# A two-layer memory transformer on one core: the weighted values of all heads in one run, and their fill

## The chip, the cores and the metric

One core of a Trainium2 chip runs the kernel. The metric is the time of one execution on the device in microseconds; lower is better.

## The reference

Two layers, each an attention with a recurrent memory and a dense block, over x of 2048 tokens by 512.

```python
def _A_ref(x, mem0, Wq, Wk, Wv, Wo, seg_len):      # 64 segments of 32 tokens, memory of M = 8 rows
    mem = mem0
    for s in range(n_seg):
        h = jnp.concatenate([mem, xs], axis=1)      # L = 40 rows
        q, k, v = (jnp.einsum('btd,dhe->bhte', h, W) for W in (Wq, Wk, Wv))   # H = 32 heads of 128
        scores = jnp.where(mask, jnp.einsum('bhqe,bhke->bhqk', q, k) * scale, -1000000000.0)
        p = _softmax(scores, axis=-1)
        o = jnp.einsum('bhqk,bhke->bhqe', p, v)
        o = jnp.einsum('bhte,hed->btd', o, Wo)
        mem = o[:, :M, :].copy()                    # the next segment's memory
        outs.append(o[:, M:, :])

x = x + _A_ref(_layernorm(x), A_mem0, A_Wq, A_Wk, A_Wv, A_Wo, A_seg_len)
x = x + relu(_layernorm(x) @ w1) @ w2               # 512 -> 1376 -> 512
# and both lines once more: layer 1, with the same weights and the same first memory
```

A segment cannot start before the memory rows of the one before it are known.

## The kernel before

**Steps.** The kernel runs 68 steps. Step k works on segment k of layer 0 (called a = 0) and on segment k - 4 of layer 1 (a = 1, `DELTA = 4`), so that two recurrences share one program; from step 4 to 63 both are there. In the attention's tiles layer 0 has partitions 0 to 39 and layer 1 has 64 to 103. The engines' programs are in the order in which the source issues them (`manual_schedule`), apart from the blocks under `high_priority`, which stand in the same order here; GpSimd is free.

**One step on TensorE.** The heads go in two halves of 16 (`hf` 0 and 1):

1. `qk` of half 0 (L663, tiles `qp`), the values of the memory rows (`memory_values`, L332, tiles `vp`), in even steps `values1(k)`, and the scores of half 0 (`scores`, L703, banks `sp0` and `sp1`). The softmax of half 0 runs beside `qk` of half 1.
2. `transpose_p` (L747, tiles `tp` into `PT`) turns the probabilities `Pf` of half 0; then the scores of half 1; then `weighted_v(0)` (L762, tiles `pv`): 32 small matmuls, 16 heads by two layers, which read `Vs` and `PT`.
3. Work that does not belong to the chain of the step, as fill: `values1(k + 1)` in even steps, `values0(k + 3)` where `fills_v0(k)` holds, part of a dense block (`dense_h`, L589, tiles `hp`; `dense_y`, L610) or of an output projection (`output_x`, L460 and L463, tiles `wox`). Meanwhile the softmax of half 1 is made: `exponents` (maximum L718 and subtraction L721 on VectorE, exponential L729 on ScalarE) and `probabilities` (sum L735, reciprocal L736 on VectorE, product L738 into `Pf`: layer 0's on GpSimd, layer 1's on VectorE).
4. `transpose_p` of half 1, a second piece of fill, `weighted_v(1)`.
5. `output_mem` (L710): 32 matmuls of `OTm`, which holds the weighted values of the memory rows, with `Wo_sb`. Fill; the sum is copied to `wm_sb` (L1073, ScalarE), turned (`mt`, L1097) and copied to `HT` (L1100, VectorE), the next step's memory rows. Fill, and the next step.

**Which fill where.** `places(i)` cuts the 32 heads of pair i's output projection: in an even step, `wx[0:2]` stands ahead of the second transposition, `wx[1:3]` behind it, `wx[2:4]` behind `output_mem`, `wx[3:5]` behind `mt`. `hs` cuts the 11 parts of `dense_h` in the same way. Even steps are of two kinds. With k = 4n, an output projection of an odd pair is the fill. With k = 4n + 2, it is `dense_h` and, from 6 to 58, `values0` (16 matmuls a call, in four column groups of the array).

**Copies out of PSUM.** `outputs_m` (L785, ScalarE) copies the memory rows of a `pv` tile to `OTm`, 8 heads a copy; `outputs_x` (L793) the others to `OTx0` or `OTx1`: ScalarE for half 0, VectorE for half 1. `ahead(k, a)` gives how many rows go to `OTm`: 8, but 24 for layer 1 in steps 4n up to 60, where 16 token rows ride along in `output_mem`. In those steps `riders_add` (L562) follows on VectorE.

**Banks.** PSUM's eight banks are `ps_c` (three buffers in turn, for `qp`, `tp`, `mt`, the memory rows' `vp` and most `pv`), `ps_fill` (two, for fill and one `pv` of each half), `ps_wo` (one) and `sp0`, `sp1`. `output_mem` sums in `sp0`. A tile that takes a buffer waits for the copies of the tile that had it. `values0` uses `ps_c` for its first product and `ps_fill` for its second, whose copy to SBUF stands behind `transpose_p` of half 1 on ScalarE (`evict_v0`).

Of the kernel before, what the change touches and what calls it, by code (L numbers as in the profile page):

```python
# [7 lines left out]
BF = mybir.dt.bfloat16  # L8
F32 = mybir.dt.float32
# [8 lines left out]
DELTA = 4  # L18
# [4 lines left out]
def kernel(  # L23
# [34 lines left out]
    wk = ctx.enter_context(tc.tile_pool(name="wk", bufs=2))  # L58
    dram = ctx.enter_context(tc.tile_pool(name="vdram", bufs=2, space=DRAM))
    ps_c = ctx.enter_context(tc.tile_pool(name="ps_c", bufs=3, space=PSUM))  # L60
    ps_s = ctx.enter_context(tc.tile_pool(name="ps_s", bufs=1, space=PSUM))
    ps_wo = ctx.enter_context(tc.tile_pool(name="ps_wo", bufs=1, space=PSUM))
    ps_fill = ctx.enter_context(tc.tile_pool(name="ps_fill", bufs=2, space=PSUM))
# [140 lines left out]
    Vs = const.tile([128, H * Dh], BF)  # L204
# [3 lines left out]
    PT = const.tile([128, 8, 2, L], BF)  # L208
    OTx0 = const.tile([128, 2, H // 2, 128], BF)
    OTx1 = const.tile([128, H // 2, 128], BF)  # L210
    OTm = const.tile([128, H, 32], BF)
    hT = const.tile([128, NFC, 128], BF)

    sp_banks, sp_tiles = [], []
    for a in range(2):
        t = ps_s.tile([128, 512], F32, name=f"sp{a}")
# [4 lines left out]
    vmds, vds = {}, {}  # L221
# [105 lines left out]
    def group_values(lhsT, ii, dst, pool, tag, q, place="VmS", later=False):  # L327
        vp = pool.tile([128, 512], F32, tag=tag, name="vp")
        for c4 in range(NC4):
            for j in range(4):  # L330
                n = 4 * ii + j
                nc.tensor.matmul(vp[32 * j:32 * j + 32, :], lhsT=lhsT(c4), rhs=Wv_sb[:, c4, n * 512:(n + 1) * 512],  # L332
                                 start=(c4 == 0), stop=(c4 == NC4 - 1), tile_position=(0, 32 * j))

        def evict():
            VmS = wk.tile([128, 512], BF, tag=place, bufs=3 if place == "VmS" else 1, name="VmS")
            nc.scalar.copy(out=VmS[:], in_=vp[:])  # L337
            q.dma_start(out=dst[ii].rearrange("j t e -> (j t) e"), in_=VmS[:])

        if later:  # L340
            return evict
        evict()
# [8 lines left out]
    def values0(s, ii):  # L351

        if ii == 0:
            vds[0, s] = dram_values("vd0", "vd0", 4)
        t = tokens_T(s, 0, SEG)
        return group_values(lambda c4: t[:, c4, :], ii, vds[0, s], *((ps_fill, "fill") if ii else (ps_c, "c")), nc.sync,
                            "xn" if ii == 1 and s > 5 else "VmS", later=ii == 1 and s > 5)

    def values1(k, ii, place="VmS"):

# [58 lines left out]
    def fills_v0(k):  # L419

        return k % 2 == 0 and k + 3 < NSEG and k + 3 not in set_of

    def places(i):

        if i % 2 == 0:
            return (0, 10, 16, 24, H), (H,) * 5
        if i == NT - 1:  # L430
            return (0, 12, 12, 12, 12), (12, H, H, H, H)
        if fills_v0(2 * i + 2):
            return (0, 6, 10, 14, 20), (20, 23, 26, 30, H)
        return (0, 6, 10, 13, 16), (16, 23, 26, 30, H)

    def output_order(i):
# [202 lines left out]
    def block_normalize(b):  # L639
        dn["b"] = wk.tile([128, Dm], BF, tag="xn", bufs=1, name="xn")  # L640
        normalize(dn["b"], R_tiles[place(b)[0]], dn["x"])
# [96 lines left out]
        eng.tensor_tensor(out=P[:, :, 64 * a:64 * a + L], in0=es[:],  # L738
                          in1=sm[:].unsqueeze(2).to_broadcast([128, 8, L]), op=ALU.mult)

    def transpose_p():

        for p, copy in ((0, nc.vector.tensor_copy), (1, nc.scalar.copy)):
            tp = ps_c.tile([128, 4, 2, L], F32, tag="c")
            for sl in range(4):
                c = PL * (4 * p + sl)
                nc.tensor.matmul(tp[:, sl], lhsT=Pf[:, c:c + 128], rhs=ident_q, start=True, stop=True)  # L747
            copy(out=PT[:, 4 * p:4 * p + 4], in_=tp[:])  # L748

    def weighted_v(hf, act):  # L750
        pvs = {}
        for q in range(2):
            h0 = 16 * hf + 8 * q
            for a in act:
                pool, tag = (ps_fill, "fill") if (hf, q, a) in ((0, 0, 0), (1, 1, 1)) else (ps_c, "c")
                pvs[q, a] = pool.tile([128, 8, L], F32, tag=tag, name="pv")
            for hh in range(8):
                sl, g2 = divmod(8 * q + hh, 2)
                h = h0 + hh
                for a in act:  # L760
                    R = 64 * a
                    nc.tensor.matmul(pvs[q, a][:, hh, :], lhsT=Vs[R:R + L, h * Dh:(h + 1) * Dh],  # L762
                                     rhs=PT[R:R + L, sl, g2, :], start=True, stop=True)
        return pvs

# [11 lines left out]
    def ahead(k, a):  # L777

        return M + 16 if a == 1 and ride_of(k) is not None and ride_of(k)[2] == 0 else M

    def outputs_m(k, hf, pvs, q):
        for a in range(2):
            if (q, a) in pvs:
                h0, n = 16 * hf + 8 * q, ahead(k, a)
                nc.scalar.copy(out=OTm[:, h0:h0 + 8, a * M:a * M + n], in_=pvs[q, a][:, :, 0:n])  # L785

    def outputs_x(k, hf, pvs, q, copy, layers=(0, 1)):
        for a in layers:
            if (q, a) in pvs:
                h0, n = 16 * hf + 8 * q, L - ahead(k, a)  # L790
                c = 64 * a + SEG * (k % 2)
                ot = OTx1 if hf else OTx0[:, k // 2 % 2]
                copy(out=ot[:, 8 * q:8 * q + 8, c:c + n], in_=pvs[q, a][:, :, L - n:L])  # L793
# [7 lines left out]
    def step(k):  # L801
        act = [a for a in range(2) if 0 <= k - a * DELTA < NSEG]
        even = k % 2 == 0
        p = k // 2
        w = p - 1 if even and p >= 1 else None
        nw = p if not even else None
        dw = p - 1 if not even and p >= 1 else None
        first = dw is not None and dw < NP
# [168 lines left out]
        wo = sp_banks[0]  # L977
        with tc.high_priority(offset=PRIO):
            transpose_p()
            scores(qks[:2], act)  # L980
            scores(qks[2:], act)
            pvs = weighted_v(0, act)

            outputs_x(k, 0, pvs, 0, nc.scalar.copy)
            outputs_m(k, 0, pvs, 0)
            ess = exponents(act)


# [10 lines left out]
        if not apart:  # L999
            v1(1)  # L1000
        with tc.high_priority(offset=PRIO):
            outputs_m(k, 0, pvs, 1)
            outputs_x(k, 0, pvs, 1, nc.scalar.copy)
        v0(0)
        evict_v0 = v0(1)
        if k == 2:
            set_values(4, 3, 5)
            set_products(4, 5)
            set_store(4, nc.sync, 2, 4)
        hs = (0, 0, 4, 8, NFC) if fills_v0(k) else (0, 6, 8, 8, NFC) if len(act) == 1 else (0, 8, NFC, NFC, NFC)  # L1010
        if sooner is not None:
            dense_h(sooner, *hs[0:2])
        final = k == NSTEP - 1
# [6 lines left out]
        with tc.high_priority(offset=PRIO):  # L1020
            for a in act:
                probabilities(1, ess, a, k)
            if first:
                hand_on(dw)
            transpose_p()
            if evict_v0 is not None:
                evict_v0()
            if k == 0:
                set_evict(3, 4)
                set_products(3, 5)  # L1030
            if k == 1:
                set_evict(4, 2)
            if k == 2:
                set_evict(4, 5)
                set_products(4, 6)
            if first:
                block_moments(dw)
# [6 lines left out]
        if nw is not None:  # L1044
            output_x(nw, *nx[1:3])
        with tc.high_priority(offset=PRIO):
            pvs = weighted_v(1, act)
            for q2 in range(2):
                if cont:
                    outputs_m(k, 1, pvs, q2)  # L1050
            head = act[:1] if nx is not None and nw % 2 == 0 else act
            outputs_x(k, 1, pvs, 0, nc.scalar.copy if final else nc.vector.tensor_copy, head)
            if first:
                block_normalize(dw)
            outputs_x(k, 1, pvs, 1, nc.vector.tensor_copy, head)
            for q2 in range(2):
                outputs_x(k, 1, pvs, q2, nc.vector.tensor_copy, [a for a in act if a not in head])
            if back is not None and place(back)[1]:
                riders_add(back)
            if dw is not None and dw >= 3 and not final:  # L1060
                store(dw)
            if k == 2:
                set_evict(4, 6)
            if k == 0:
                set_evict(3, 5)
                set_values(3, 6, 7)
                output_mem(wo, 0, 24)
                set_values(3, 7, 8)
                output_mem(wo, 24, H)
            elif cont:  # L1070
                output_mem(wo, 0, H)
            if cont:
                nc.scalar.copy(out=wm_sb[:], in_=wo[:])  # L1073
            if k == 0:
                set_products(4, 0)
            if k == 2:
                set_products(4, 7)
# [125 lines left out]
```

## Time and profile before

| | |
|---|---|
| median of 3 runs | 1613.6 us (1612.4 to 1614.39) |
| the profiled execution | 1612.95 us; its span 1611.2 us |
| TensorE (PE) busy | 1597.3 us, 37172 matmuls |
| VectorE (DVE) busy | 1082.3 us |
| ScalarE (ACT) busy | 859.1 us |
| GpSimd (POOL) busy | 267.6 us |
| HBM | 69 GB/s over the span |

PE stands for matmuls, PEld for the loads of their stationary operand. The ends of matmuls are modelled and overlap, so what is read off here are their starts. A step takes some 22 to 24 us. A wait before a matmul is booked on the weight load ahead of it where that load reads what was waited for.

### The profile page before, as it was taken

The page shows a single profiled execution, that of the slowest core. Times are in us where ns is not written, and L with a number is a line of the kernel's source. Part 1 is how long each engine was busy: PE and PEld are TensorE (multiplying, and loading weights), DVE is VectorE, ACT ScalarE, POOL GpSimd, SP SyncE. Part 2 cuts the span into 40 slices and gives each one's busy share as a digit, 9 for nine tenths or more (in the row PEclk, how much of TensorE's full clock was granted, in tenths as well). Part 3 has the DMA queues.
Part 4 walks back from the last instruction along what each step waited for, and adds up shares of the span by engine and source line. Part 5 has one row for each costly group of instructions (what it writes and reads, how often), then busy time and mean ns, then how long its engine had stood idle before and what let it go on. Part 6 is the DMA issues. An engine that isn't in the chain of part 4 may idle for free.

```text
span 1611.2 us, 83133 instructions
## 1 busy us (share of the span) xinstructions
PE 1597.3 (99%) x37172; PEld 1175.3 (73%) x37172; DVE 1082.3 (67%) x2603; ACT 859.1 (53%) x2422; POOL 267.6 (17%) x510
## 2 busy tenths in 40 slices
PE   9999999999999999999999999999999999999998
PEld 4677777677777767777777777777777777777766
DVE  5556766776776677677667767666766767676655
ACT  4455555555555555555555555555555555555544
POOL 1112111111211111121111112111111211111100
PEclk9999999999999999999999999999999999999999
DMA  9732222222222222222322222222222222221111
GB/s 343 265 116 65 69 75 67 68 60 66 63 70 80 67 67 63 62 63 70 80 67 67 63 61 63 72 78 69 69 58 63 61 75 73 67 61 52 51 44 37
DMA packets 138309, 126.09 MB, mean 78 GB/s; under 512 B 43928, under 2 KB 126976, under 8 KB 137088
## 3 DMA queue, kind: packets, MB, share of 16 engines
q1 hardware_dynamic: 135296, 116.55, 24.8%
q8 instruction: 291, 4.77, 1.3%
q0 software_dynamic: 2560, 4.20, 1.0%
q14 instruction: 66, 0.54, 0.1%
q10 hardware_dynamic: 96, 0.04, 0.0%
HBM read 65.94 MB, written 45.35 MB: 69 GB/s over the span
## 4 chain that ended last, share of the span: by engine, by line
PE 95%; DVE 2%; DMA 1%; issue 1%; ACT 1%; POOL 0%; SPq 0%; DVEq 0%; ACTq 0%; POOLq 0%
PE qp L663 37%; PE vp L332 16%; PE sp L710 8%; PE wox L460 7%; PE hp L589 5%; PE yp L610 5%; PE pv L762 4%; PE wox L463 4%; PE sp L703 4%; PE tp L747 3%; PE vp L303 2%; DMA Wv_sb<-in_A_Wv_dram 0%; PE mt L1097 0%; PE tpx L648 0%; DVE PT L748 0%
## 5 line engine op out<-in xcount | busy, mean ns | idle before, releaser
L663 PE MATMUL qp<-HT,Wq_sb 128*128 128x80 bf16 (+1 forms) x8704 | 368.6, 199 | 0.9 <-DVE HT L1100 0.9
L663 PE MATMUL qp<-HT,Wk_sb 128*128 128x80 bf16 (+1 forms) x8704 | 367.7, 199 | 0.0
L663 PEld LDWEIGHTS <-Wq_sb 128*128 128x128 bf16 x8704 | 328.4, 99 | 19.9 <-issue 11.0
L663 PEld LDWEIGHTS <-Wk_sb 128*128 128x128 bf16 x8704 | 329.7, 99 | 0.8
L669 DVE CAST KT<-qp 128x480 bf16<-128x480 f32 (+3 forms) x340 | 199.4, 586 | 169.5 <-PE qp L663 163.5
L667 ACT CAST QT<-qp 128x480 bf16<-128x480 f32 (+3 forms) x340 | 172.4, 507 | 206.9 <-PE qp L663 206.1
L738 POOL TENSOR_TENSOR Pf<-es,sm 128x320 bf16<-128x320 f32 x187 | 135.3, 723 | 621.2 <-ACT QT L667 353.0
L337 ACT CAST VmS<-vp 128x512 bf16<-128x512 f32 x290 | 167.4, 588 | 117.6 <-PE vp L332 117.5
L718 DVE TENSOR_REDUCE mx<-sp 128x8 f32<-128x320 f32 x256 | 114.5, 486 | 115.6 <-PE sp L703 115.2
L729 ACT ACTIVATE es<-es 128x320 f32<-128x320 f32 x256 | 111.0, 469 | 75.3 <-DVE es L721 69.2
L735 DVE TENSOR_REDUCE sm<-es 128x8 f32<-128x320 f32 x256 | 120.5, 471 | 23.5 <-ACT es L729 13.0
L710 PE MATMUL sp<-Wo_sb,OTm 128*32 128x512 bf16 x2144 | 128.2, 380 | 0.0
L332 PE MATMUL vp<-Wv_sb,rT 128*32 128x512 bf16 x2144 | 128.0, 380 | 0.1
L460 PE MATMUL wox<-Wo_sb,OTx 128*128 128x512 bf16 x480 | 122.8, 380 | 0.0
L332 PE MATMUL vp<-Wv_sb,HT 128*32 128x512 bf16 x2048 | 122.5, 380 | 0.0
L721 DVE TENSOR_TENSOR es<-sp,mx 128x320 f32<-128x320 f32 x256 | 113.1, 480 | 0.5
L231 POOL TENSOR_TENSOR rstd<-rstd,mhalf_t 128x1 f32<-128x1 f32 x85 | 47.0, 553 | 397.9 <-DVE rstd L230 397.9
L793 DVE CAST OTx<-pv 128x256 bf16<-128x256 f32 x255 | 85.3, 385 | 36.5 <-ACT OTm L785 35.7
L785 ACT CAST OTm<-pv 128x64 bf16<-128x64 f32 x510 | 92.9, 252 | 30.9 <-PE pv L762 30.9
L748 ACT CAST PT<-tp 128x320 bf16<-128x320 f32 x136 | 58.3, 429 | 72.3 <-PE tp L747 70.1
L793 ACT CAST OTx<-pv 128x256 bf16<-128x256 f32 (+1 forms) x257 | 79.0, 362 | 28.6 <-PE pv L762 28.6
L748 DVE CAST PT<-tp 128x320 bf16<-128x320 f32 x136 | 66.8, 491 | 38.3 <-PE tp L747 37.2
(138 smaller groups left out, 1934.0 us busy)
## 6 DMA issues: line engine op xcount, KB each, us to landing
vd<-VmS SPq DMA_DIRECT2D x156, 128.0 KB
Vs<-vd SPq DMA_DIRECT2D x156, 128.0 KB
vmd<-VmS SPq DMA_DIRECT2D x134, 128.0 KB
Vs<-vmd SPq DMA_DIRECT2D x254, 32.0 KB
Vs<-vmd SPq DMA_DIRECT2D x120, 64.0 KB
Vs<-vset SPq DMA_DIRECT2D x19, 256.0 KB
Wv_sb<-in_A_Wv_dram SPq DMA_DIRECT2D x4, 1024.0 KB
Wq_sb<-in_A_Wq_dram SPq DMA_DIRECT2D x4, 1024.0 KB
```

The costliest lines, as they stand in the source:

```text
L332: nc.tensor.matmul(vp[32 * j:32 * j + 32, :], lhsT=lhsT(c4), rhs=Wv_sb[:, c4, n * 512:(n + 1) * 512], start=(c4 == 0), stop=(c4 == NC4 - 1 ...
L337: nc.scalar.copy(out=VmS[:], in_=vp[:])
L460: nc.tensor.matmul(wo_tiles[i][:], lhsT=ot, rhs=Wo_sb[:, h, :], start=(n == 0), stop=(n == H - 1))
L663: nc.tensor.matmul(qp[:, hi, 0:ncol], lhsT=W_sb[:, c4, h * Dh:(h + 1) * Dh], rhs=HT[:, c4, a_lo:a_hi, :], start=(c4 == 0), stop=(c4 == NC4 ...
L667: nc.scalar.copy(out=dst[:, 0:nh, a_lo * L:a_hi * L], in_=qp[:, 0:nh, 0:ncol])
L669: nc.vector.tensor_copy(out=dst[:, 0:nh, a_lo * L:a_hi * L], in_=qp[:, 0:nh, 0:ncol])
L710: nc.tensor.matmul(wo[32 * j:32 * j + 32, :], lhsT=OTm[:, h, :], rhs=Wo_sb[:, h, :], start=(h < 4), stop=(h >= H - 4), tile_position=(0, 3 ...
L718: nc.vector.tensor_reduce(out=mxs[a][:], in_=sp_tiles[a], axis=AX.X, op=ALU.max)
L735: nc.vector.tensor_reduce(out=sm[:], in_=es[:], axis=AX.X, op=ALU.add)
L738: eng.tensor_tensor(out=P[:, :, 64 * a:64 * a + L], in0=es[:], in1=sm[:].unsqueeze(2).to_broadcast([128, 8, L]), op=ALU.mult)
L748: copy(out=PT[:, 4 * p:4 * p + 4], in_=tp[:])
L793: copy(out=ot[:, 8 * q:8 * q + 8, c:c + n], in_=pvs[q, a][:, :, L - n:L])
```

## The change

Even steps from 4 to 60 (`joint(k)`) no longer weigh half 0's values by themselves. `transpose_p` of half 1 writes a tile of its own (`PT1`), and behind it `joint_v` weighs all 32 heads of both layers in one run of 64 matmuls. The run fills six tiles of up to 12 heads, one for each (j, a), in `ps_c`, `ps_fill`, `sp1` and, in steps 4n + 2, `ps_wo`. `joint_m` copies the memory rows to `OTm`: the first twelve heads of layer 1 on VectorE, the others on ScalarE. `joint_x` copies the rest, all but one tile on VectorE.

The fill moves with it. In steps 4n nine heads of the output projection stand ahead of the second transposition and one behind it, where there were seven and three. In steps 4n + 2 one part of `dense_h` (4 matmuls) stands ahead of it and three behind, where there were none and four. `values0`'s second product goes to `ps_c`, and its copy is no longer put behind the transposition.

```diff
 def values0(s, ii):
-        return group_values(lambda c4: t[:, c4, :], ii, vds[0, s], *((ps_fill, "fill") if ii else (ps_c, "c")), nc.sync,
-                            "xn" if ii == 1 and s > 5 else "VmS", later=ii == 1 and s > 5)
+        return group_values(lambda c4: t[:, c4, :], ii, vds[0, s],
+                            *((ps_fill, "fill") if ii and not joint(s - 3) else (ps_c, "c")), nc.sync,
+                            "xn" if ii == 1 and s > 5 else "VmS", later=ii == 1 and s > 5 and not joint(s - 3))
...
+    def joint(k):
+        return k % 2 == 0 and DELTA <= k < NSEG - 2
...
 def places(i):
-        if fills_v0(2 * i + 2):
-            return (0, 6, 10, 14, 20), (20, 23, 26, 30, H)
+        if joint(2 * i + 2):
+            return (0, 6, 10, 13, 16), (16, 25, 26, 30, H)
         return (0, 6, 10, 13, 16), (16, 23, 26, 30, H)
...
-    def transpose_p():
+    PTs = {}
+
+    def transpose_p(hf=0, apart=False):
+        PTs[hf] = wk.tile([128, 8, 2, L], BF, tag="es", bufs=2, name="PT1") if apart else PT
...
+    def joint_v(k):
+        pvs = {}
+        for j in range(3):
+            for a in range(2):
+                if (j, a) == (1, 1):
+                    t = sp_banks[1]
+                else:
+                    where = (ps_c, "c") if (j, a) in ((0, 0), (2, 0), (2, 1)) else (ps_fill, "fill")
+                    if k % 4 == 2 and (j, a) == (0, 1):
+                        where = (ps_wo, "wo")
+                    t = where[0].tile([128, 512], F32, tag=where[1], name="pv")
+                pvs[j, a] = t[:, 0:12 * L].rearrange("p (h l) -> p h l", h=12)
+        for h in range(H):
+            hf, (sl, g2) = h // 16, divmod(h % 16, 2)
+            for a in range(2):
+                R = 64 * a
+                shared = (h // 12, a) == (1, 1)
+                nc.tensor.matmul(pvs[h // 12, a][:, h % 12, :], lhsT=Vs[R:R + L, h * Dh:(h + 1) * Dh],
+                                 rhs=PTs[hf][R:R + L, sl, g2, :], start=not shared or h == 12, stop=True,
+                                 skip_group_check=shared)
+        return pvs
+
+    def joint_m(k, pvs, j, a, copy):
+        h0, h1, n = 12 * j, min(12 * j + 12, H), ahead(k, a)
+        copy(out=OTm[:, h0:h1, a * M:a * M + n], in_=pvs[j, a][:, 0:h1 - h0, 0:n])
+
+    def joint_x(k, pvs, j, a, copy):
+        h0, h1, n = 12 * j, min(12 * j + 12, H), L - ahead(k, a)
+        c = 64 * a + SEG * (k % 2)
+        for ot, lo, hi in ((OTx0[:, k // 2 % 2], 0, 16), (OTx1, 16, H)):
+            u, v = max(h0, lo), min(h1, hi)
+            if u < v:
+                copy(out=ot[:, u - lo:v - lo, c:c + n], in_=pvs[j, a][:, u - h0:v - h0, L - n:L])
...
-            pvs = weighted_v(0, act)
-            outputs_x(k, 0, pvs, 0, nc.scalar.copy)
-            outputs_m(k, 0, pvs, 0)
+            if not joint(k):
+                pvs = weighted_v(0, act)
+                outputs_x(k, 0, pvs, 0, nc.scalar.copy)
+                outputs_m(k, 0, pvs, 0)
             ess = exponents(act)
...
-            outputs_m(k, 0, pvs, 1)
-            outputs_x(k, 0, pvs, 1, nc.scalar.copy)
+            if not joint(k):
+                outputs_m(k, 0, pvs, 1)
+                outputs_x(k, 0, pvs, 1, nc.scalar.copy)
...
-        hs = (0, 0, 4, 8, NFC) if fills_v0(k) else (0, 6, 8, 8, NFC) if len(act) == 1 else (0, 8, NFC, NFC, NFC)
+        hs = (0, 1, 4, 8, NFC) if joint(k) else (0, 0, 4, 8, NFC) if fills_v0(k) else (0, 6, 8, 8, NFC) if len(act) == 1 else (0, 8, NFC, NFC, NFC)
...
-            transpose_p()
+            transpose_p(1, joint(k))
...
-            pvs = weighted_v(1, act)
+            if joint(k):
+                pvs = joint_v(k)
+                joint_m(k, pvs, 0, 1, nc.vector.tensor_copy)
+                for j, a in ((0, 0), (1, 0), (1, 1), (2, 0), (2, 1)):
+                    joint_m(k, pvs, j, a, nc.scalar.copy)
+                for j in range(3):
+                    for a in range(2):
+                        joint_x(k, pvs, j, a, nc.scalar.copy if (j, a) == (2, 0) else nc.vector.tensor_copy)
+            else:
+                pvs = weighted_v(1, act)
...
```

More of the change, by code (lines that the diff above doesn't have):

```diff
@@ L747, in transpose_p @@
                 nc.tensor.matmul(tp[:, sl], lhsT=Pf[:, c:c + 128], rhs=ident_q, start=True, stop=True)
-            copy(out=PT[:, 4 * p:4 * p + 4], in_=tp[:])
+            copy(out=PTs[hf][:, 4 * p:4 * p + 4], in_=tp[:])
     def weighted_v(hf, act):
@@ L762, in weighted_v @@
                     nc.tensor.matmul(pvs[q, a][:, hh, :], lhsT=Vs[R:R + L, h * Dh:(h + 1) * Dh],
-                                     rhs=PT[R:R + L, sl, g2, :], start=True, stop=True)
+                                     rhs=PTs[hf][R:R + L, sl, g2, :], start=True, stop=True)
         return pvs
+    def joint_v(k):
[29 more added lines that the diff above has]
+                copy(out=ot[:, u - lo:v - lo, c:c + n], in_=pvs[j, a][:, u - h0:v - h0, L - n:L])
     def ride_of(k):
@@ L1046, in step @@
         with tc.high_priority(offset=PRIO):
-            pvs = weighted_v(1, act)
[L1048 to L1057, printed above, removed]
+            if joint(k):
[8 more added lines that the diff above has]
+                pvs = weighted_v(1, act)
+                for q2 in range(2):
+                    if cont:
+                        outputs_m(k, 1, pvs, q2)
+                head = act[:1] if nx is not None and nw % 2 == 0 else act
+                outputs_x(k, 1, pvs, 0, nc.scalar.copy if final else nc.vector.tensor_copy, head)
+                if first:
+                    block_normalize(dw)
+                outputs_x(k, 1, pvs, 1, nc.vector.tensor_copy, head)
+                for q2 in range(2):
+                    outputs_x(k, 1, pvs, q2, nc.vector.tensor_copy, [a for a in act if a not in head])
             if back is not None and place(back)[1]:
```

## The prediction

> **What bounds the kernel now.** I read the page first: busy shares and the chain.
>
> ```profile
> PE 1597.3 (99%) x37172; PEld 1175.3 (73%) x37172; DVE 1082.3 (67%) x2603; ACT 859.1 (53%) x2422; POOL 267.6 (17%) x510
> PE 95%; DVE 2%; DMA 1%; issue 1%; ACT 1%; POOL 0%; SPq 0%; DVEq 0%; ACTq 0%; POOLq 0%
> ```
>
> TensorE sets the end, and its program runs in a fixed order. The change keeps all its 37172 matmuls. So it can gain or lose only where TensorE stands still: on a wait, or where it passes from one shape of matmul to another. Next I read the waits of the weight loads, since a matmul's wait shows there.
>
> ```profile
> PEld L747 <- POOL Pf L738: 9.5, 19, 1.1
> ```
>
> 19 times the transposition of the probabilities (L747) waited for them. The timeline of step 26 (k = 4n+2, the kind with dense_h and values0) shows how they are made:
>
> ```profile
> 644.26 0.64 PE L762 MATMUL pv<-PT,Vs 40*128 40x40 bf16 x32
> 644.39 0.89 DVE L718 TENSOR_REDUCE mx<-sp 128x8 f32<-128x320 f32 x2 [0.21 <-PE sp L703]
> 644.83 1.91 PE L332 MATMUL vp<-Wv_sb,HT 128*32 128x512 bf16 x32
> 645.20 0.88 DVE L721 TENSOR_TENSOR es<-sp,mx 128x320 f32<-128x320 f32 x2
> 645.71 0.87 ACT L729 ACTIVATE es<-es 128x320 f32<-128x320 f32 x2
> 646.21 0.48 DVE L735 TENSOR_REDUCE sm<-es 128x8 f32<-128x320 f32 x1
> 647.56 0.62 DVE L738 TENSOR_TENSOR Pf<-es,sm 128x320 bf16<-128x320 f32 x1
> 648.40 0.46 PE L747 MATMUL tp<-ident,Pf 128*128 128x80 bf16 x8
> 648.69 1.06 PE L589 MATMUL hp<-dnT,w_sb 128*128 128x128 bf16 x16
> 649.68 0.59 PE L762 MATMUL pv<-PT,Vs 40*128 40x40 bf16 x32
> 649.79 0.60 ACT L595 ACTIVATE hT<-hp 128x512 bf16<-128x512 f32 x1
> 650.20 0.40 PE L710 MATMUL sp<-Wo_sb,OTm 128*32 128x512 bf16 x4
> ```
>
> Columns: start, duration, instruction. Call S the first TensorE instruction after half 1's scores, here 644.26. Half 0's weighted values end at S+0.57, values1 and values0 at S+4.13, where the second transposition begins. The softmax of half 1 runs beside them and ends at 647.56+0.62 = S+3.92. Nothing waits here, by about 0.1 us. Step 24 (k = 4n, S = 595.91) has only values1 and seven wox as cover:
>
> ```profile
> 599.20 0.62 DVE L738 TENSOR_TENSOR Pf<-es,sm 128x320 bf16<-128x320 f32 x1
> 599.89 0.34 PEld L747 LDWEIGHTS <-Pf 128*128 128x128 bf16 x8 [0.40 <-POOL Pf L738]
> 599.93 0.45 PE L747 MATMUL tp<-ident,Pf 128*128 128x80 bf16 x8
> 600.21 0.81 PE L460 MATMUL wox<-Wo_sb,OTx 128*128 128x512 bf16 x3
> 600.95 0.63 PE L762 MATMUL pv<-PT,Vs 40*128 40x40 bf16 x32
> 601.51 1.70 PE L710 MATMUL sp<-Wo_sb,OTm 128*32 128x512 bf16 x28
> ```
>
> Again the softmax ends at S+3.91, and the transposition starts 0.10 us later, at S+4.02: it waited, if only some 0.09 us (the last wox stands 0.309 us before it, its spacing is 0.216). In the steps looked at, 4 to 60, the softmax ends at S+3.92 in all but two.
>
> **The change part by part.** It touches 29 steps: 15 of kind 4n (4 to 60), 14 of kind 4n+2 (6 to 58). I follow each kind from S to the first L710, output_mem, which starts the recurrence's tail; what follows that keeps its order.
>
> (a) Removed before the transposition: one run of 32 pv, S to S+0.57. Of this 0.41 us is work (16 pairs of 25.3 ns, read from the starts inside the run), the rest change of shape. The work comes back behind the transposition; the 0.16 us of change does not.
>
> (b) Moved ahead of it: four dense_h matmuls (4 x 0.056 = 0.22 us) in 4n+2, two wox (0.43) in 4n. Cover is now: 4n+2, 3.57 (values, 644.83 to 648.40) + 0.22 = 3.79; 4n, 1.84 (values1) + 9 x 0.216 = 3.78. Both fall short of the softmax, S+3.92, by 0.13 us plus the 0.10 from its end to the matmul. Could the softmax end earlier? ACT is relieved of eight copies there, but each exp follows the DVE subtraction that feeds it (ACT idle 0.11 us before the first, released by DVE), and the rest stands on DVE, which loses nothing in this stretch. So the transposition starts at S+4.02 in both kinds: 0.11 us sooner than before in 4n+2, unchanged in 4n. The removed run turns into a stall. Behind the waiting weight load stand the joint run, output_mem and the whole next step.
>
> (c) Behind the transposition, 4n+2: 0.28 (8 tp) + 0.77 (12 of the 16 hp: 0.99 - 4 x 0.056) puts the joint run J at S+5.07. The run takes the 0.52 of a run of 32 plus 16 x 0.0253 = 0.92: S+5.99. Before: 4.13 + 0.29 + 0.99 + 0.52 = S+5.94. In 4n: 0.28 + 0.31 (one wox and the 0.096 that the change to pv costs) gives J = S+4.61; before, pv began at S+5.04 and output_mem at S+5.61 (601.51, rounded up).
>
> (d) Output_mem's first head now needs two copies of twelve heads: ACT's (layer 0, 96 elements a row) and DVE's (layer 1: 96 in 4n+2, 288 in 4n, where ahead() is 24). Behind output_mem's waiting weight load stand its other 31, mt and the next step's qk. The copies can start when the 24th pv is done: J+0.29, plus 0.21 until DVE starts (as the HT copy does after its matmul) = J+0.51. DVE's cost for 288 is not in the trace. Nearest rows: HT 64 elements 0.225 us, OTx 128 0.28, OTx 256 0.42, PT 320 0.49. On that line 288 costs 0.45; bounds 0.23 to 0.49. Its end, J+0.96, plus the 0.10 from a DVE end to a matmul that loads its result: J+1.07, while the run ends at J+0.92. So 4n pays 0.15 us here (0 to 0.19). In 4n+2 DVE's 96 elements (0.25) are ready in time; ACT's stand behind the ReLU of L595, which begins 0.10 us into the run and lasts 0.60; ACT overlaps its next by 0.10, so the copy runs J+0.60 to J+0.83, and output_mem starts at J+0.94, 0.02 late (up to 0.12 if they do not overlap).
>
> Before, output_mem waited for copies too, but for eight heads, the first half of them long done. The Trainium skill, TensorEngine Tiling, "PSUM Bottleneck", warns that packing matmuls does not speed up the emptying of PSUM. By that rule alone this wait would be the bound; the rows give it 0.02 and 0.15 us.
>
> (e) Sum: 4n+2, 4.02+0.28+0.77+0.94 = S+6.01 against 5.94, +0.07, times 14 = +0.9. 4n, 4.02+0.28+0.31+1.07 = S+5.68 against 5.61, +0.07, times 15 = +1.1. Together +2.0 us.
>
> (f) At nothing. The eviction tail: in 4n DVE has after J+0.96 seven copies (about 1.04 ns an element after each other, as L793's 256 follow every 0.33 us and its 128 every 0.20: 1.8 us) and riders_add (0.69): done by J+3.5. The next HT copy is due when mt is done, 2.72+0.27 us after output_mem starts: J+4.06. Spare 0.6; in 4n+2, 0.6 too. Banks: values0's second product waits for PT's copy, over 2 us earlier, and the joint tiles for VmS copies that end by S+4.3, before J. SP: the stores of values0 are issued a little sooner; the next step's loads of half 0 are issued after the joint run instead of after the first run, 2 to 5 us later (at 599.64 in step 24, before), but their reader comes some 15 us later. xn: values0's copy is now ahead of the PT copy on ACT (0.59 us, S+3.7 to S+4.3); the transposition's copy is due at S+4.5. dnT, which hp now needs at S+3.57, lands by S+3.2 in the worst step (14).
>
> The profiled execution took 1612.95 us (span 1611.2), the runs' median is 1613.6; +2.0 on the median gives 1615.6.
>
> **Rivals.** A: *the removed run pays.* Its case is the drain: the last values matmul stands 0.309 to 0.312 us before a full-array one, against 0.216 within a run, so 0.09 us for each change of shape, and the change drops one in 29 steps. If half 1's softmax ends 0.2 us sooner, with DVE undisturbed by ACT, the natural starts S+3.79 and S+3.78 hold: 14 x 0.22 + 15 x 0.24 = 6.6 us less than my sum, -4.6: 1609.0. Half of that gives 1612.3. Against it: P ends at S+3.92 in both kinds though ACT does different copies. The Trainium skill, TensorEngine Tiling, "Key Properties", has this rule: changing the tiling mode drains the array. By that rule the change gains; the trace agrees on the drain (0.09 us), and by it alone, 29 x 0.09, the time would be 1611.
>
> B: *output_mem waits longer.* TensorE is held by the two copies of the first twelve heads. With the upper ends of (d), 15 x 0.04 + 14 x 0.10 = 2.0 more, +4.0: 1617.6. It decides from output_mem at J+1.11 in 4n and J+0.98 in 4n+2, where the sum passes +3.2. For it: both copies are in forms that the trace lacks.
>
> C: *the late DVE copies reach HT.* If the seven do not overlap (2.4 us for 1.8) and each waits for ACT's copy of its bank, DVE is done at J+4.05 in 4n, when HT is due, and from there each 0.1 us costs 1.5 us, as the first qp there already follows HT at once (0.05 us): at 0.1 late, with the sum above, 1617.1; at 0.2, 1618.6.
>
> D: *the copies are not late*, DVE's 288 at 0.30 us or less: -2.2 in 4n, -0.3 in 4n+2: 1613.1.
>
> **How the numbers follow.** The forecast's mechanism 0.50 (1614.2 to 1617.0), A 0.17 (1609.0 to 1612.3), B 0.15, C 0.08 (1617.1 to 1618.6), D 0.10. About 0.2%, 3.2 us, is what a measurement here can tell from no change: below 1610.4 or above 1616.8. Faster: two thirds of A, 0.12. Slower: B, C and a tenth of the forecast, 0.28. Same: 0.60. The range leaves out the end of A and the end of C: 1610.5 to 1618.5.
>
> **What would show it.** Right: the transposition starts at S+4.02 in all joint steps, its weight load waiting for Pf some 0.2 us, in 29 steps or more; pv runs of 64 last 0.9 us; output_mem starts J+1.07 in 4n, behind a DVE OTm copy of about 0.45, and J+0.94 in 4n+2; HT still follows mt at once. Wrong: a softmax end before S+3.8 (A), output_mem beyond J+1.11 (B), qp waiting for an HT that stood behind OTx copies (C).

## The result, and the profile after

The changed kernel takes 1618.71 us (median of 6 runs, 1617.99 to 1619.56), the kernel before beside it 1613.43 (6 runs, 1612.4 to 1614.39). The ratio is 1.0034, 95% interval 1.0023 to 1.0044: slower by 5.3 us, where 2.0 were forecast; 0.2 us above the range. The profiled execution took 1619.36 us, its span is 1617.7.

The page after, busy shares and the chain:

```profile
PE 1598.8 (99%) x37172; PEld 1176.1 (73%) x37172; DVE 1115.7 (69%) x2719; ACT 830.8 (51%) x2248; POOL 267.0 (17%) x510
PE 92%; DVE 2%; issue 2%; ACT 1%; POOL 1%; DMA 0%; SPq 0%; ACTq 0%; DVEq 0%; POOLq 0%
```

TensorE's share of the chain falls from 95 to 92%, with the same 37172 matmuls: it stands still more. VectorE does 33 us more work and ScalarE 28 us less, which is the move of the copies. Step 24 (k = 4n, S = 598.49), from the timeline, with lines left out:

```profile
601.78 0.62 DVE L745 TENSOR_TENSOR Pf<-es,sm 128x320 bf16<-128x320 f32 x1
...
602.51 0.34 PEld L758 LDWEIGHTS <-Pf 128*128 128x128 bf16 x8 [0.56 <-POOL rT L1151]
602.54 0.45 PE L758 MATMUL tp<-ident,Pf 128*128 128x80 bf16 x8
...
603.64 0.58 ACT L805 CAST OTm<-pv 128x96 bf16<-128x96 f32 x2
...
603.68 0.46 DVE L805 CAST OTm<-pv 128x288 bf16<-128x288 f32 x1 [0.23 <-PE pv L798]
...
604.25 0.36 PEld L717 LDWEIGHTS <-OTm 128*32 128x32 bf16 x12 [0.20 <-ACT OTm L805]
604.28 0.61 PE L717 MATMUL sp<-Wo_sb,OTm 128*32 128x512 bf16 x8
```

Two stalls are seen. The transposition (L758) starts at 602.545, though its input ends at 602.399; the releaser named, POOL's `rT`, is a bystander, as `rT` is not read there: the product on VectorE is what came last. And output_mem (L717) starts at 604.285, with VectorE's copy done at 604.138 and ScalarE's long before. Both prices are the same, 0.146 and 0.147 us. Step 26 (k = 4n + 2, S = 647.07, J = 652.18), first on TensorE, then the copies ahead of output_mem:

```profile
650.64 0.40 PE L596 MATMUL hp<-dnT,w_sb 128*128 128x128 bf16 x4
651.13 0.45 PE L758 MATMUL tp<-ident,Pf 128*128 128x80 bf16 x8
...
652.18 0.49 PE L798 MATMUL pv<-PT,Vs 40*128 40x40 bf16 x25
...
653.12 1.24 PE L717 MATMUL sp<-Wo_sb,OTm 128*32 128x512 bf16 x17
```

```profile
652.28 0.60 ACT L602 ACTIVATE hT<-hp 128x512 bf16<-128x512 f32 x1 [0.19 <-PE hp L596]
652.72 0.26 DVE L805 CAST OTm<-pv 128x96 bf16<-128x96 f32 x1 [0.69 <-PE pv L798]
652.78 0.45 ACT L805 CAST OTm<-pv 128x96 bf16<-128x96 f32 x2
```

VectorE's copy ends at 652.976 (J+0.80) and output_mem starts at 653.123, again 0.147 us behind it, as in all 14 steps of this kind. ScalarE's first copy (the row joins two), behind the ReLU, had ended at J+0.83.

Measured against the forecast, in us from S; J is the start of the joint run (steps 8 to 60):

| | 4n forecast | 4n after | 4n+2 forecast | 4n+2 after |
|---|---|---|---|---|
| softmax ends | 3.92 | 3.91 | 3.92 | 3.92 |
| transposition | 4.02 | 4.06 | 4.02 | 4.06 |
| joint run J | 4.61 | 4.66 | 5.07 | 5.11 |
| output_mem | 5.68 (J+1.07) | 5.80 (J+1.14) | 6.01 (J+0.94) | 6.06 (J+0.94) |
| output_mem before | 5.61 | | 5.94 | |

From output_mem to the next step's first `qp` nothing changes (0.00 us). Added up step by step against the trace of before, 6.4 of the span's 6.5 us are: steps 4n +2.8, steps 4n + 2 +1.3 (step 6 alone is 0.2 faster), odd steps +1.4, the start of the program and steps 0 to 3 -0.6, and 1.5 in step 4. The last belongs to this execution. The windows around it (busy time of PE, PEld, DVE, ACT and POOL, TensorE's granted clock, DMA share, GB/s):

```profile
125.00:132.00 7.00, 5.88 (x164) 3.48 (x164) 5.42 (x15) 3.87 (x12) 1.46 (x3) 1.00 0.33 55
132.00:135.40 3.40, 3.40 (x34) 1.22 (x28) 1.35 (x7) 0.80 (x4) 0.00 (x0) 0.50 0.53 154
```

Output_mem of step 4 in the timeline, of this kernel and then of one that differs only in a tile's place (e1_own_tile below) and has the full clock there:

```profile
131.71 3.38 PE L717 MATMUL sp<-Wo_sb,OTm 128*32 128x512 bf16 x32 [0.17 <-ACT OTm L805]
```

```profile
132.29 1.91 PE L717 MATMUL sp<-Wo_sb,OTm 128*32 128x512 bf16 x32 [0.17 <-ACT OTm L809]
```

The clock was 0.50 for 3.4 us, and the 32 matmuls took 3.38 us instead of 1.91. None of the other 15 kernels' profiled executions shows it in step 4, so it is left out of what follows. The Trainium skill, TensorE: Matmul & The Clock Gate, "What's actually happening", gives half the clock and a window of 3413 ns for it; this row agrees, 0.50 and 3.413 us in the clock's own record. What set it off here was not tried; in the 7 us ahead of it TensorE was busy for 5.88 us and stood still for at most 0.96 us at a stretch.

### The profile page after: what moved, and what is told of

Read it like the earlier page. It is cut to its first block, busy times and chain, and to the rows that moved or that the text cites. A ratio compares the mean times of both kernels' runs of the same rounds, so it can differ in the third digit from the quotient of the medians.

```text
span 1617.7 us, 83147 instructions
## 1 busy us (share of the span) xinstructions
PE 1598.8 (99%) x37172; PEld 1176.1 (73%) x37172; DVE 1115.7 (69%) x2719; ACT 830.8 (51%) x2248; POOL 267.0 (17%) x510
## 4 chain that ended last, share of the span: by engine, by line
PE 92%; DVE 2%; issue 2%; ACT 1%; POOL 1%; DMA 0%; SPq 0%; ACTq 0%; DVEq 0%; POOLq 0%
PE qp L670 38%; PE vp L332 14%; PE sp L717 8%; PE wox L467 5%; PE hp L596 5%; PE yp L617 5%; PE wox L470 4%; PE sp L710 4%; PE tp L758 3%; PE pv L773 3%; PE vp L303 2%; PE pv L798 1%; POOL Pf L745 1%; DVE es L728 1%; ACT es L736 1%
## 5 line engine op out<-in xcount | busy, mean ns | idle before, releaser
L337 ACT CAST VmS<-vp 128x512 bf16<-128x512 f32 x290 | 164.0, 585 | 117.8 <-PE vp L332 116.4
L717 PE MATMUL sp<-Wo_sb,OTm 128*32 128x512 bf16 x2144 | 129.6, 383 | 1.9 <-ACT OTm L805 0.2
L596 PE MATMUL hp<-dnT,w_sb 128*128 128x128 bf16 (+2 forms) x1452 | 90.5, 217 | 0.2 <-ACT VmS L337 0.2
L596 PEld LDWEIGHTS <-w_sb 128*128 128x128 bf16 (+1 forms) x1452 | 80.0, 100 | 13.3 <-issue 12.7
L717 PEld LDWEIGHTS <-OTm 128*32 128x32 bf16 x2144 | 54.6, 97 | 47.7 <-ACT OTm L805 3.3
```

Source lines behind the costliest of these rows:

```text
L596: nc.tensor.matmul(hp[0:fs, fi, r0:r1], lhsT=w1_sb[:, c4, fc * 128:fc * 128 + fs], rhs=xnT[:, c4, r0:r1], start=(c4 == 0), stop=(c4 == NC4 ...
L717: nc.tensor.matmul(wo[32 * j:32 * j + 32, :], lhsT=OTm[:, h, :], rhs=Wo_sb[:, h, :], start=(h < 4), stop=(h >= H - 4), tile_position=(0, 3 ...
```

## The experiments

All 14 are edits of the changed kernel, but for one of the kernel before, and each was timed beside the kernel before.

**Which steps carry it.** Three kernels do the change in fewer steps.

```diff
-        return k % 2 == 0 and DELTA <= k < NSEG - 2
+        return k % 2 == 0 and DELTA < k < NSEG - 2     # e2_from6
+        return k % 4 == 0 and DELTA <= k < NSEG - 2    # e3_only4n
+        return k % 4 == 2 and DELTA <= k < NSEG - 2    # e4_only4n2
```

> Joint from step 6 on: step 4 is as in the kernel before. Theory, the clock dip: in the changed kernel's trace TensorE's clock fell to half for 3.4 us in step 4, which cost 1.5 us on top of a wait of some 0.3; without it the time falls by 1.7 us to about 1617.0 if every run had the dip, and the trace shows none. Rival, the dip is an accident of the profiled run: about 0.3 us less, 1618.4.

1618.50 us, ratio 1.0032 (1.0019 to 1.0044). Step 4 comes back to its old length, but it was worth only 0.3 us without the clock's drop. The drop belonged to one execution, as the rival had it.

> Joint in steps 4n alone, with their fill; steps 4n+2 as before, values0 with its old banks. Theory, waits: 15 x 0.19 in the joint steps + 15 x 0.036 in the odd ones behind + the 1.5 us of step 4 if its clock falls: +3.4 without the dip, +4.9 with it, 1616.8 or 1618.3. Rival, one cost spread over all steps or made in 4n+2: under +2, 1615.4 or less.

1618.51 us, 1.0036 (1.0022 to 1.005); the runs spread over 3.5 us. In its trace the 15 steps cost 3.5 us, 4n + 2 0.3, odd steps 0.5. The profiled execution, 1617.11, was the fastest of the five, so 1.4 us of the median does not show in the trace.

> Joint in steps 4n+2 alone, with their fill and values0's banks; steps 4n as before. Theory, waits: 14 x 0.12 + 14 x 0.058 = +2.5, 1615.9, no dip of the clock. Rival, that values0's banks or its earlier copy cost more than the joint run: +4 or more, and waits at values0 or at the copies of PT in the trace.

1616.72 us, 1.002 (1.0011 to 1.0029). In its trace the 14 steps cost 1.35 us, the odd steps behind them 1.0 (0.06 each), and unchanged steps 4n 1.7, in single waits of up to 0.9 us in a few of them. Each kind keeps its price without the other, +0.19 in most steps 4n and +0.12 in a step 4n + 2, and the odd step after each pays too. The medians agree only roughly with these sums (4.7 and 2.9 us over the kernel before, 7.6 together, where the whole change costs 5.3): single waits, of which more below, differ from kernel to kernel.

**The odd steps.** Nothing in the forecast touched them. They lose 0.036 us after a step 4n and 0.058 after 4n + 2, always between the first `qp` and the first transposition. In step 27, ScalarE's two exponentials and the QT copy that gives a `ps_c` bank back, after:

```profile
664.90 0.93 ACT L736 ACTIVATE es<-es 128x320 f32<-128x320 f32 x2 [0.98 <-DVE es L728]
...
666.51 0.56 ACT L674 CAST QT<-qp 128x480 bf16<-128x480 f32 x1 [0.24 <-PE qp L670]
```

`PT1` takes a buffer of `es`. So the next step's second exponential, which writes in place there, has to wait for ScalarE's own copy to PT1 besides VectorE's subtraction. The program has a separate wait instruction ahead of it, and the pair takes 0.93 us instead of 0.87. The edit below puts PT1's halves into a KT and a QT buffer.

```diff
-        PTs[hf] = wk.tile([128, 8, 2, L], BF, tag="es", bufs=2, name="PT1") if apart else PT
+        if apart:
+            PTs[hf] = [wk.tile([128, HB, 2 * L], BF, tag=tag, bufs=3, name="PT1")[:, 0:4].rearrange(...)
+                       for tag in ("KT", "QT")]
```

> PT1 no longer takes a buffer of the exponentials (es); its two halves take a KT and a QT buffer, which are idle there. Theory, waits in three places: the odd step after a joint one loses its 0.036 us (4n+1) and 0.058 us (4n+3), since its second exp no longer waits for two engines; 14 to 15 steps of each, so 1.4 us less than the changed kernel, about 1617.3; the joint steps keep their +0.19 and +0.12. Rival, that the odd steps are slowed by the late DVE copies or by the loads of Vs that now come together: no change in the odd steps, 1618.7.

The same lines of that kernel:

```profile
663.47 0.87 ACT L736 ACTIVATE es<-es 128x320 f32<-128x320 f32 x2 [1.03 <-DVE es L728]
...
665.09 0.56 ACT L674 CAST QT<-qp 128x480 bf16<-128x480 f32 x1 [0.30 <-PE qp L670]
```

The pair takes 0.87 again and the odd steps lose 0.06 us in all instead of 1.43. So the mechanism is shown. But the median is 1618.49, ratio 1.0031 (1.0019 to 1.0043): no gain. The trace tells where it went: steps 30, 34 and 38 lose 0.8 us more than in the changed kernel. Step 38's maximum, of the changed kernel (S = 930.73) and of this one (S = 929.34):

```profile
930.86 0.89 DVE L725 TENSOR_REDUCE mx<-sp 128x8 f32<-128x320 f32 x2 [0.21 <-PE sp L710]
```

```profile
929.82 0.89 DVE L725 TENSOR_REDUCE mx<-sp 128x8 f32<-128x320 f32 x2 [0.56 <-PE sp L710]
```

The releases that it waits for come within 0.1 us of S in both; VectorE starts 0.13 and 0.48 us behind S. In step 30 it is VectorE's subtraction that is 0.14 to 0.16 us late, in step 34 ScalarE's exponential of half 0, by 0.27. All three are late in the four kernels with PT1 in these buffers (e9_best, e11_best_first_wait and e14_best_no_swap below) and in none of the other twelve. So these waits go with PT1's place and not with the run; what they are was not found.

**The place of the fill.** If TensorE stands still ahead of the transposition whatever is there, fill that stays behind it is paid in full.

```diff
-            return (0, 6, 10, 13, 16), (16, 25, 26, 30, H)
+            return (0, 6, 10, 13, 16), (16, 23, 26, 30, H)      # e8; e5 and e12: (16, 26, 26, 30, H)
-        hs = (0, 1, 4, 8, NFC) if joint(k) ...
+        hs = (0, 0, 4, 8, NFC) if joint(k) ...                  # e8; e5: (0, 4, ...), e12: (0, 2, ...)
```

> The changed kernel with the fill where it was before: seven wox ahead of the transposition and three behind in 4n, no dense_h ahead and sixteen behind in 4n+2. Theory 1, the transposition cannot start before S+4.06 whatever stands ahead of it, so fill that stands behind it is paid in full: J moves 2 x 0.216 = 0.43 us later in 4n and 0.22 us in 4n+2, 15 x 0.43 + 14 x 0.22 = +9.5 us on the changed kernel's 1618.6: 1628. Rival, J is later but output_mem does not wait for the copies as it does now (they are no nearer to J), so this only adds and stays within +9 to +10; or the softmax is delayed by the fill itself (weight loads of wox read SBUF while VectorE works): then the transposition starts earlier than S+4.06 with less fill ahead, and the time is 1622 to 1625.

1629.55 us, 1.01 (1.0086 to 1.0113). The transposition stays at S+4.06, output_mem moves to S+6.24 and S+6.28: the first theory, step by step. The move of the fill is thus worth 10.8 us; without it the joint run would cost 16.

> All fill of the stretch stands ahead of the second transposition in the 29 joint steps: ten wox in steps 4n (nine and one in the changed kernel), sixteen dense_h matmuls in 4n+2 (four and twelve). Theory 1, the time goes where TensorE stands still, once at the transposition (softmax, S+4.06) and once more at output_mem: in 4n the tenth wox brings the natural start to 1.84 + 10 x 0.216 + 0.09 = S+4.09, so no stall is left there; J falls to S+4.37, heads 16 and up wait for PT1's DVE copy, which ends 0.90 us behind the first tp (S+4.99), and output_mem comes at about S+5.55 to 5.60 instead of 5.80, -0.2 to -0.25 x 15 = -3.0 to -3.8. In 4n+2 the transposition moves to S+4.56, PT1's copies stand in the way of the run and output_mem comes at about S+6.0 instead of 6.06, -0.1 to 0 x 14. Together 1614.0 to 1616.0. Rival, the wait only moves: the joint run stalls at head 16 for the same time that the stall ahead of the transposition loses, and output_mem stays at S+5.80: 1618 to 1619.

1615.58 us, 1.0014 (1.0005 to 1.0022): output_mem at S+5.61 in 4n, where before had it, and at S+6.02 in 4n + 2. There is a limit to it: in both kinds the last pv now comes at J+1.06 instead of J+0.84 and J+0.80, since head 16 waits for PT1's copies.

> The changed kernel with other cuts of the fill alone: ten wox ahead in 4n, two parts of dense_h ahead in 4n+2. Theory, the cuts decide the even steps: 4n output_mem at S+5.60 (0 against before), 4n+2 at J+0.94 with J = S+4.89 to 4.93, S+5.83 to 5.87 (-0.09 x 14 = -1.2), odd steps as in the changed kernel (+1.4): 1613.5 to 1614.5. Rival, 4n+2 stays at S+6.02, as where all four parts stood ahead, because PT1's copies hold the run: 1615.5.

1613.15 us, 1.0000 (0.9991 to 1.0009): level with before. 4n at S+5.61, 4n + 2 at S+5.84 (0.10 under before), odd steps as in the changed kernel.

**The price from VectorE's end to the matmul.** Forecast at 0.10, measured at 0.147, twice a step in 4n. The trace's records show a separate wait instruction ahead of the weight load, where a matmul has to wait for two engines: one wait stands on it, the other on the load. For the transposition of step 24 after:

```profile
L758 PEldq EVENT_SEMAPHORE  x1: 51/51/51, 602.4 to 602.4; - x1
```

With VectorE's wait on this instruction, it starts some 0.04 us after VectorE's end, lasts 0.051, and the load follows. In the first test the engines of the first two OTm copies are swapped, so ScalarE comes last.

```diff
-                joint_m(k, pvs, 0, 1, nc.vector.tensor_copy)
-                for j, a in ((0, 0), (1, 0), (1, 1), (2, 0), (2, 1)):
+                joint_m(k, pvs, 0, 0, nc.vector.tensor_copy)
+                for j, a in ((0, 1), (1, 0), (1, 1), (2, 0), (2, 1)):
```

> Only the engines of the first two OTm copies change places: VectorE copies layer 0's first twelve heads (96 elements a row), ScalarE layer 1's (288 in 4n). Theory 1, output_mem's wait in 4n is DVE's 288 copy (0.458 us) plus 0.147 us from DVE's end to the matmul: ScalarE starts at J+0.50 and copies 288 in 0.405, and if from its end to a matmul it takes 0.10 us, output_mem starts at J+1.01 instead of J+1.143, -0.13 x 15 = -2.0 us; 4n+2 keeps J+0.94, as ScalarE's copy there is of 96 elements in both. 1616.5 to 1617.0. Rival, the 0.147 belongs to TensorE's first matmul of a new shape, whoever releases it: J+1.06, -0.08 x 15 = -1.2: 1617.5. Rival, output_mem's later heads are then late, since ScalarE has the other four copies behind a longer one: J+1.14 or more and gaps inside output_mem, 1618.5 or over.

1615.89 us, 1.0016 (1.0008 to 1.0025). Step 24 of its timeline (J = 601.46):

```profile
601.96 0.26 DVE L805 CAST OTm<-pv 128x96 bf16<-128x96 f32 x1 [0.20 <-PE pv L798]
602.00 0.54 ACT L805 CAST OTm<-pv 128x288 bf16<-128x288 f32 x2 [0.17 <-PE pv L798]
...
602.45 0.40 PE L717 MATMUL sp<-Wo_sb,OTm 128*32 128x512 bf16 x4
```

ScalarE's first copy (the row joins two) ends at 602.394, output_mem starts 0.053 us later, at J+0.99 instead of J+1.14; 4n + 2 gains 0.03, to J+0.91. The separate wait, for VectorE, was over earlier. 15 x 0.15 + 14 x 0.03 = 2.7 us, 2.8 in the medians. The second test is to let VectorE come last, but with its wait on the load itself.

```diff
             tp = ps_c.tile([128, 4, 2, L], F32, tag="c")
+            if apart and p == 0:
+                nc.tensor.matmul(tp[0:L, 0, 0], lhsT=Pf[:, 0:L], rhs=ident_q[:, 0], start=True, stop=True)
             for sl in range(4):
```

> The changed kernel with one more matmul ahead of each second transposition of the joint steps: 40 columns of Pf, GpSimd's part alone, into a corner of tp that the next matmul writes anew. So the wait for GpSimd stands on that matmul, and the transposition's own weight load has one wait left, for VectorE's product, with no separate instruction for it. Theory, the 0.147 us from VectorE's end to the matmul is the separate wait instruction, which takes 0.051 us behind its release, and the wait on the weight load itself costs 0.053, as output_mem's did behind ScalarE's copy in the swapped kernel: the transposition starts at S+3.97 instead of S+4.06, -0.09 x 29 = -2.6 us: 1616.0. Rival, VectorE's results reach TensorE later than ScalarE's, whatever instruction waits: S+4.06 stays, 1618.6. Rival, the added matmul's other shape costs a change of mode (0.09): S+4.06 again, but with the weight load starting earlier.

1618.41 us, 1.0031 (1.0019 to 1.0042); step 24:

```profile
601.60 0.62 DVE L745 TENSOR_TENSOR Pf<-es,sm 128x320 bf16<-128x320 f32 x1
...
602.19 0.20 PE L757 MATMUL tp<-ident,Pf 128*40 128x40 bf16 x1
...
602.32 0.35 PE L760 MATMUL tp<-ident,Pf 128*128 128x80 bf16 x5
```

From VectorE's end, 602.219, to the transposition, 602.316, it is 0.097 us. But VectorE does not set this start. The added matmul starts at S+3.89, where its fill ends, and the transposition follows 0.129 us behind it; so it is in 27 of the 29 steps. In e11_best_first_wait below, step 24 has the same 0.129 with VectorE done at 600.155, 0.3 us earlier:

```profile
600.34 0.20 PE L761 MATMUL tp<-ident,Pf 128*40 128x40 bf16 x1
...
600.47 0.46 PE L764 MATMUL tp<-ident,Pf 128*128 128x80 bf16 x8
```

Only in four steps does VectorE's end come last: 4 and 6 here, 4 and 38 in e11_best_first_wait. Step 4 here, where VectorE ends at 131.159:

```profile
130.54 0.62 DVE L745 TENSOR_TENSOR Pf<-es,sm 128x320 bf16<-128x320 f32 x1
...
131.22 0.46 PE L760 MATMUL tp<-ident,Pf 128*128 128x80 bf16 x8 [0.15 <-DVE Pf L745]
```

In all four the transposition starts 0.056 or 0.057 us behind VectorE, nearly the 0.053 behind ScalarE. So the theory is right on the price, in four steps: the separate wait instruction is 0.09 of the 0.147, and the two engines hardly differ. What keeps the gain small is what the last rival names, the added matmul itself: 0.129 us until the next one may start, against 0.035 between two of the transposition's own. Output_mem comes 0.03 earlier, 0.8 us in 29 steps, less than these medians resolve.

**The banks of values0 alone**, in the kernel before.

```diff
-                            *((ps_fill, "fill") if ii else (ps_c, "c")), nc.sync, ... later=ii == 1 and s > 5)
+                            *((ps_fill, "fill") if ii and not joint(s - 3) else (ps_c, "c")), nc.sync, ...
+                            later=ii == 1 and s > 5 and not joint(s - 3))
```

> The kernel before with one part of the change alone: values0's second product in steps 6 to 58 of kind 4n+2 uses ps_c, and its copy stands ahead of the transposition's on ScalarE. No joint run. Theory 1, as forecast, this part costs nothing: S to output_mem stays 5.935 in 4n+2 and the odd steps keep their length, 1613.0 to 1614.2. Rival, it carries part of the loss, because the ps_c buffer comes free later for tp, or because the early copy delays the softmax's exponentials on ScalarE: +0.1 us in each of 14 steps, 1615 or over.

1623.94 us, 1.0061 (1.0047 to 1.0075): the loss that the rival expected, but seven times its size, and at another wait. The reason stands in its timeline of step 26, where the second product of values0 waits for half 0's OTx copy on ScalarE, 0.67 us a step:

```profile
651.86 0.68 ACT L797 CAST OTx<-pv 128x256 bf16<-128x256 f32 x2
652.31 1.05 PE L332 MATMUL vp<-Wv_sb,xnT 128*32 128x512 bf16 x16 [0.49 <-ACT OTx L797]
```

The joint run takes that `pv` tile out of `ps_c`, and with it this wait. The part costs nothing in the changed kernel because of the other part; the two can't be priced one by one.

**All together.** PT1 as in e1_own_tile, the copies as in e6_swap, the cuts as in e12_cuts.

> Four edits of the changed kernel together: PT1 in KT's and QT's buffers instead of es; the first two OTm copies swapped; in 4n all ten wox ahead of the transposition; in 4n+2 two parts of dense_h ahead of it and two behind (one and three in the changed kernel). Theory, the costs are separate and each belongs to its place: the odd steps lose nothing; 4n has output_mem at S+5.60, as the run with all fill ahead; in 4n+2 the natural start rises to 3.79 + 0.22 = S+4.01, with the drain S+4.1, so no stall is left, eight hp behind it give J = S+4.89 to 4.93, and output_mem at J+0.91 = S+5.80 to 5.84 against 5.935 before. Sum against before: 0 x 15 - 0.12 x 14 = -1.7: 1611.5 to 1613. Rival, in 4n+2 PT1's copies now hold the joint run at head 16 (first copy ends 0.90 us behind the first tp, S+5.0, its reader is due at J+0.41 = S+5.30, so it should not): output_mem at S+6.0 and 1614.5.

1610.88 us, 0.9983 (0.9974 to 0.9992): faster than both kernels, by 0.17% against the one before. Output_mem at S+5.54 in 4n (5.61 before) and S+5.80 in 4n + 2 (5.94). Taking single edits back:

> The kernel of the four edits with PT1 back in the es buffers, as in the changed kernel. Theory, PT1 in es costs the odd steps 0.036 us after a step 4n and 0.058 after a step 4n+2, in the median as in the trace: 15 x 0.036 + 14 x 0.058 = 1.4 us: 1612.3, against 1610.9 with all four. Rival, the odd steps' loss is given back later in the step or is hidden by single waits, as the first run with PT1 moved alone showed no gain in its median: 1610.5 to 1611.2.

1612.89 us, 0.9992 (0.9984 to 1.0001). So PT1 in `es` costs 2.0 us in the median too (1.5 by the ratios, whose intervals still overlap). Against that kernel its trace has 1.6 in the odd steps, 0.9 in 4n (S+5.60; with PT1 in one tile head 16 waits longer), and -0.6 in 4n + 2, in the three steps named above.

> The kernel of the four edits with the first two OTm copies as in the changed kernel: layer 1's on VectorE, layer 0's on ScalarE. Theory, output_mem then waits for VectorE last again, in 4n from S+5.54 to S+5.61 and in 4n+2 from S+5.80 to S+5.83 (the run with the cuts alone had 5.607 and 5.836): 15 x 0.07 + 14 x 0.03 = 1.5 us: 1612.4. Rival, with the transposition's copies holding the run in 4n, the swap is worth nothing there: 1611.3.

1612.05 us, 0.9991 (0.9982 to 1.0000): 1.2 us for the swap by the medians, less than the ratios' intervals resolve; in the trace S+5.59 and S+5.84, 15 x 0.05 + 14 x 0.03.

> The four edits together and the added matmul. If the separate wait instruction costs 0.09 us: in 4n the transposition and PT1's copies, which hold the run there, move 0.09 us sooner unless the tenth wox now ends later (natural start S+4.09), so 0 to -0.09 x 15; in 4n+2 the fill ends at S+4.01 to 4.1 by itself, so nothing. 0 to -1.3 us against the four edits alone: 1610.5 to 1613. If not, the same time as those.

1615.83 us, 1.0013 (1.0004 to 1.0021), 5 us more than without the added matmul. In e9_best the last wox of step 24 starts at S+3.80 and the transposition at S+4.07, where a spacing of 0.216 would have it at S+4.01: some 0.05 us of stall is left to hide it. The added matmul starts 0.309 us behind the last wox and the transposition 0.129 behind that, and output_mem moves 0.18 to 0.20 us later in most steps: one matmul of another shape, paid nearly in full.

## Why the forecast was wrong

**(a) Removed run.** Right. The softmax ends at S+3.91 and S+3.92, though ScalarE has eight copies less, so the time of the removed run turned into a stall.

**(b) The transposition at S+4.02.** The step that failed is "the 0.10 from its end to the matmul". It is 0.147 here, with VectorE's wait on a separate instruction. The row it was read from, step 24 of before, has 0.10 with that instruction waiting for two things: there its record had begun 2.5 us before and ended 0.046 us behind VectorE, where after it begins 0.039 behind VectorE and lasts 0.051. Step 62 of before, whose row was not looked at, has 0.146. 0.05 us in 29 steps: 1.3 us.

**(c) J and the joint run.** Right but for what (b) hands on: 0.60 and 1.05 us from the transposition to J, 0.80 to 0.84 to the last pv.

**(d) Output_mem.** In 4n+2 the start, J+0.94, came out by luck. The forecast had it behind ScalarE's copy, which did end at J+0.83. But by the 0.053 us of e6_swap that copy would have let it start at J+0.88, before the J+0.91 that the run allowed there. What held it is VectorE's copy, which the forecast had ready in time: it started at J+0.54 instead of J+0.51, ended at J+0.80 and cost 0.147. In 4n VectorE's 288 elements took 0.458 us (0.45 forecast) and started at J+0.54 (0.51); the rest is the same 0.10 again, which is 0.147. J+1.14 instead of J+1.07: 15 x 0.07 = 1.1 us.

**(e) Sum.** Forecast 2.0; with these two terms 4.4, and 4.1 measured without the clock's drop (step 6 gains, and in steps 12 and 48 before had a wait of its own). **(f) At nothing.** VectorE's tail, SP, xn and dnT did cost nothing. What the list lacked is PT1's place: 1.4 us in the odd steps, a term that the forecast left out. With the 4.1 it makes 5.5 in the trace, against 5.3 by the medians. Two sums of the forecast are slightly off, J+0.96 + 0.10 (J+1.06) and A's 14 x 0.22 + 15 x 0.24 (6.7); neither matters to the outcome.

**Rivals.** A failed on the softmax. The drain that it counted on is real, as the added matmul showed with some 0.18 us a step where little covers it (the Trainium skill, TensorEngine Tiling, "Key Properties", by which a change of mode drains the array: agrees). But the changed kernel saves it inside a stall. B was half right: output_mem passed its point J+1.11 in 4n, and stayed at J+0.94, under J+0.98, in 4n + 2, though held by VectorE there too. C fell: HT follows mt as before. D fell: 0.458 us.

## What to carry to other kernels

Work that is taken from ahead of a wait gives nothing until the wait itself moves: first count what covers it, and move as much fill ahead as the wait is long, no more (here two parts of dense_h beyond that, some 0.45 us, cost 0.18 us in each step 4n + 2). A price "from engine to matmul" is read from a row with the same waits, and a tile put in another's buffer is costed in the next step that uses that buffer. Where two engines release one instruction, see which of them comes last and on which instruction its wait stands, even where the start comes out as forecast. And where an added instruction is to test a wait, check first that it does not set the start by itself.

## What the hardware showed that was not expected

- From a release to TensorE's matmul: 0.147 us behind VectorE where the wait stands on a separate instruction (all 29 joint steps), 0.056 to 0.057 on the weight load itself (four steps of e10_first_wait and e11_best_first_wait), 0.053 behind ScalarE on the weight load (e6_swap).
- One 128x40 matmul between 128x128 ones starts 0.309 us behind a wox, where a wox follows another every 0.216, and the next starts 0.129 behind it (e11_best_first_wait).
- On ScalarE one more wait ahead of an exponential put it and the copy behind it 0.06 us back, and TensorE lost as much some 1 us later.
- In steps 30, 34 and 38, one instruction of VectorE or ScalarE starts 0.14 to 0.35 us late, in all four kernels with PT1 in the KT and QT buffers and in no other. They take 0.8 us in the trace of e1_own_tile, which differs from the changed kernel by one tile's place. Their cause stays open.
